# Value products in chunks of 128 tokens, with one chunk mixed from both batches

## The chip, the cores and the metric

The kernel runs on one core of a Trainium2 chip. The metric is the device time of one execution in microseconds (us), median of several runs. The engines are TensorE (PE, and PEld for its weight loads), VectorE (DVE), ScalarE (ACT), GpSimd (POOL) and SyncE (SP, which issues most DMAs). A matrix product has a stationary operand, which a weight load brings into the array (its columns become the partitions of the result), and a moving operand that streams past it (its columns become the columns of the result). Both are read over up to 128 partitions, the contraction.

## The reference, cut to what matters

Two batches of 448 tokens (`seq`) go through attention, then a block with a Fourier mixing and two dense layers, then the gated block that the change is about:

```python
def _moe2_ref(x, w_in, g_ln, w_sg, b_sg, w_out):        # x: (2, 448, 768)
    h = x @ w_in                                        # 768 -> 1024
    c = np.float32(np.sqrt(2.0 / np.pi))
    h = 0.5 * h * (1.0 + np.tanh(c * (h + 0.044715 * h ** 3)))
    d_ff = h.shape[-1]
    u, v = (h[..., :d_ff // 2], h[..., d_ff // 2:])     # 512 each
    mu = np.mean(v, axis=-1, keepdims=True)
    var = np.mean((v - mu) ** 2, axis=-1, keepdims=True)
    v_n = (v - mu) / np.sqrt(var + 1e-06) * g_ln
    v_s = np.einsum('ts,bsd->btd', w_sg, v_n) + b_sg[None, :, None]
    gated = u * v_s
    return (x + gated @ w_out).astype(np.float32)
```

The gate `w_sg` (448 by 448) mixes tokens, so `v_n` has to lie with tokens on partitions, while `u` and `x` lie with channels on partitions.

## The kernel before, in words

Every float32 product is made as three products: each operand is split into a high part that TensorE takes in one pass (`F32R`) and a rest, and `product()` (lines 134 to 141) adds high by high, high by rest and rest by high into one PSUM bank. So a contraction over `n` blocks is `3 n` weight loads and `3 n` matrix products.

The first 200 us hold attention and the Fourier block. Then line 1131 loops over six groups `g` of the dense layers: `hidden` (72 products of 448 columns a batch, "h") and `mixed` (72 a batch, "c"). In the last group `mixed` also splits its result into `x2[b]`, channels on partitions, six blocks of 448 tokens, high and rest. The gated block follows from line 1164:

- `gate_inputs(b)`: "u", four blocks of 128 channels, 18 products of 448 columns each; then the activation `gelu2`.
- `gate_values(b)`: "v", four chunks of 112 tokens (`CP`, `NT`). For each chunk 36 products: the stationary operand is the chunk's 112 tokens of `x2`, the moving one 256 columns of `w_in`. Then `gelu2`, mean and variance over the 512 channels, and the split into `vn[t]`, tokens on partitions. The six steps on VectorE and three on ScalarE of a chunk cover 112 partitions by 512 columns.
- `gate(b)`: "sg", four blocks `d` of 128 channels: 12 products each, contraction over the four chunks of 112 tokens, moving operand `sgT` (the gate, transposed and split, 112 partitions by 4 by 448). VectorE scales by `g_half`, adds `b_half` and multiplies by `ug[d]`; ScalarE and VectorE split that into `gated`.
- `project(b)`: "out", six blocks of 12 products, an add into `xT` on VectorE, four transposes "xt" a block, a copy on ScalarE and a DMA to the result.

Their order in the program is: u of batch 0, v of 0, u of 1, sg of 0, v of 1, `project` of 0 (six steps), sg of 1, the rest of `project` of 0, `project` of 1. A scheduler turns the program into one instruction order for each engine when the kernel is built; it may put an instruction that it expects to be ready ahead of one that it expects to wait. Engines then run their orders strictly, with semaphores between them. Dependences are followed for parts of a tile.

PSUM has eight banks. From line 992 on, four are two "big" tiles of two banks (only `hidden` uses them, through `big_ps`), and four form a ring that `one_ps` hands out in turn to everything else.

`sgT` is made in group 3 (lines 1146 to 1153): for each of four blocks of 112 rows of `w_sg` a DMA into the one buffer `sg_raw`, four transposes into a bank of the ring, and a split by ScalarE and VectorE into `sgT`. All four blocks share the one buffer, so each load after the first waits until the transposes of the block before have read it.

Of the kernel before, what the change touches and what calls it, by code (L numbers as in the profile page):

```python
# [12 lines left out]
F32 = mybir.dt.float32  # L13
F32R = mybir.dt.float32r
# [3 lines left out]
ALU = mybir.AluOpType  # L18
# [3 lines left out]
P = 128  # L22
B, H, S, D = 2, 12, 448, 64
C = H * D
NP = H // 2
CP = S // 4
NT = 4
FF1 = 4 * C
NF = FF1 // P
NG = 6  # L30
# [60 lines left out]
def attention_mixers_kernel(ctx, tc, bounded, q, k, v, cap, w_ch1, w_ch2, w_in, g_ln, w_sg, b_sg, w_out,  # L91
# [76 lines left out]

    xT = [keep.tile([P, NP, S], F32, name=f"xT{b}") for b in range(B)]
    normed = [None, None]  # L170


    def fourier(b, fp, t2sb, pool_folds=()):
# [83 lines left out]
    def layer_norm(b, fp):  # L257

        u = xT[b]

        def channel_sum(half, src, tag):
            vec.tensor_tensor(half, src[0], src[1], op=ALU.add)
            acc = fp.tile([P, S], F32, tag="acc", name=f"acc_{tag}{b}")
            vec.tensor_tensor(acc, half[:, 0, :], half[:, 1, :], op=ALU.add)
            vec.tensor_tensor(acc, acc, half[:, 2, :], op=ALU.add)
            return acc

        t = SimpleNamespace(d=[], sq=[])

        def total():  # L270
            half = fp.tile([P, 3, S + 2], F32, tag="y", bufs=2, name=f"half{b}")[:, :, :S]
            t.acc = channel_sum(half, (u[:, 0:3, :], u[:, 3:6, :]), "m")

        def mean():
            t.mu = two_ps(f"mu{b}", 1)[0]
            pe.matmul(t.mu[:, :S], mean_w, t.acc, start=True, stop=True)

        def centre():
            for i in range(2):
                d = fp.tile([P, 3, S], F32, tag="d", bufs=2, name=f"d{b}_{i}")  # L280
                vec.tensor_tensor(d, u[:, 3 * i:3 * i + 3, :], t.mu[:, :S].unsqueeze(1).to_broadcast([P, 3, S]),
                                  op=ALU.subtract)
                t.d.append(d)

        def square():
            for i in range(2):
                q2 = fp.tile([P, 3, S + 2], F32, tag="y", bufs=2, name=f"sq{b}_{i}")[:, :, :S]
                act.activation(q2, t.d[i], AF.Square)
                t.sq.append(q2)

        def square_total():
            t.acc2 = channel_sum(t.sq[0], t.sq, "v")

        def variance():
            t.vps = two_ps(f"var{b}", 1)[0]
            if bounded and not b:
                stream(t.vps, 12)
            for i in range(NT):
                pe.matmul(t.vps[:CP, 2 * i:2 * i + 2], t.acc2[:, i * CP:(i + 1) * CP], mean_w[:, 0:2],
                          start=True, stop=True)  # L300

        def deviation():
            var = small.tile([CP, NT], F32, tag="var", name=f"varc{b}")
            vec.tensor_scalar(var, t.vps[:CP, 0:2 * NT:2], 1e-6, None, op0=ALU.add)
            t.rstd = small.tile([CP, NT], F32, tag="rstd", name=f"rstd{b}")
            pool.tensor_tensor(t.rstd, var, neg_half[:CP, :NT], op=ALU.pow)

        def row():
            t.rps = two_ps(f"rstdrow{b}", 1)[0]
            if bounded and b:  # L310
                stream(t.rps, 12)
            for i in range(NT):
                pe.matmul(t.rps[:, i * CP:(i + 1) * CP], t.rstd[:, i:i + 1].to_broadcast([CP, P]), ident[:CP, :CP],
                          start=True, stop=True)

        def scale(c):
            part = lambda c: t.d[c // 3][:, c % 3, :]
            if c == 0:
                un[b] = normed[b].tile([P, 2, NP, S], F32R, tag="normed", name=f"un{b}")
            if c < NP:  # L320
                vec.tensor_tensor(part(c), part(c), t.rps[:, :S], op=ALU.mult)
            if 0 < c <= NP:
                act.copy(un[b][:, 0, c - 1, :], part(c - 1))
            if c > 1:
                vec.tensor_tensor(un[b][:, 1, c - 2, :], part(c - 2), f32(un[b][:, 0, c - 2, :]), op=ALU.subtract)  # L325

        return SimpleNamespace(total=total, mean=mean, centre=centre, square=square, square_total=square_total,
                               variance=variance, deviation=deviation, row=row, scale=scale)
# [466 lines left out]
    def gate_values(b, gp, x2, wv):  # L795

        vn = []

        def normalise(t, gv, mv):
            tc.keep_in_program_order(  # L800
                vec.tensor_scalar(gv, gv, mv[:, 0:1], mv[:, 1:2], op0=ALU.subtract, op1=ALU.mult))
            w = hpool[b].tile([P, 2, 512], F32R, tag="h", bufs=4, name=f"vn{b}_{t}")[:CP]
            split(w[:, 0], w[:, 1], gv)
            vn.append(w)

        last = None
        for t in range(NT):
            ps = one_ps(f"v{b}_{t}")
            for j in range(2):
                product(ps[:CP, j * 256:(j + 1) * 256], lambda n, a: x2[:, a, n, t * CP:(t + 1) * CP],  # L810
                        lambda n, a: wv[2 * j + n // 3][:, a, n % 3, :], NP)
            gv = gp.tile([P, DH], F32, tag="gv", bufs=3, name=f"gv{b}_{t}")[:CP]
            gelu2(gp, gv, ps[:CP, :], CP, f"v{b}_{t}", last)
            st = small.tile([P, 6], F32, tag="bst", name=f"bst{b}_{t}")[:CP]
            vec.bn_stats(st, gv)
            mv = small.tile([P, 2], F32, tag="bag", name=f"bag{b}_{t}")[:CP]
            vec.bn_aggr(mv, st)

            vec.tensor_scalar(mv[:, 1:2], mv[:, 1:2], 4e-6, None, op0=ALU.add)  # L819
            pool.tensor_tensor(mv[:, 1:2], mv[:, 1:2], neg_half[:CP, 0:1], op=ALU.pow)  # L820
            last = functools.partial(normalise, t, gv, mv)
        last()
        return vn

    def gate_inputs(b, gp, x2, wu):
# [6 lines left out]
            ug.append(g)  # L832
        return ug

    def gate(b, gp, vn, ug, sgT, g_half, b_half):
        gated = normed[b].tile([P, 2, ND, S], F32R, tag="normed", name=f"gated{b}")
        for d in range(ND):
            ps = one_ps(f"sg{b}_{d}")
            product(ps[:, :S], lambda n, a: vn[n][:, a, d * P:(d + 1) * P], lambda n, a: sgT[:, a, n, :], NT)
            tmp = gp.tile([P, S], F32, tag="gelu", bufs=3, name=f"gate{b}_{d}")  # L840
            vec.scalar_tensor_tensor(tmp, ps[:, :S], g_half[:, d:d + 1], b_half, op0=ALU.mult, op1=ALU.add)
            vec.tensor_tensor(tmp, tmp, ug[d], op=ALU.mult)
            split(gated[:, 0, d, :], gated[:, 1, d, :], tmp)
        return gated
# [279 lines left out]
    if not bounded:  # L1124
        run(mixed(1, 0, hs1, w2, None))
    sp_pool = ctx.enter_context(tc.tile_pool(name="spatial", bufs=1, side="right"))
    sgT = sp_pool.tile([CP, 2, NT, S], F32R, name="sgT", bufs=1)
    g_half = sp_pool.tile([P, GATE_ROW // 4], F32, name="g_half", bufs=1)[:, :ND]
    b_half = sp_pool.tile([P, S], F32, name="b_half", bufs=1)
    x2 = [None] * B  # L1130
    for g in range(1, NG):
        if g == 1:
            if bounded:
# [6 lines left out]
        else:  # L1140
            w1 = [columns(w_ch1, g * GF + f, "w1_") for f in range(GF)]
            hs = [[], []]
            for b in range(B):
                run(hidden(b, g, un, w1, hs[b]))
        if g == 3:
            for c in range(NT):
                sg_raw = sp_pool.tile([P, S], F32, tag="sgraw", bufs=1, name=f"sg_raw{c}")[:CP]
                sp.dma_start(sg_raw, w_sg[c * CP:(c + 1) * CP, :])
                ps = one_ps(f"sgT{c}")
                for t in range(NT):  # L1150
                    pe.transpose(ps[:CP, t * CP:(t + 1) * CP], sg_raw[:, t * CP:(t + 1) * CP], ident[:CP, :CP])
                src = ps[:CP, :S].rearrange("p (t x) -> p t x", t=NT)
                split(sgT[:, 0, :, c * CP:(c + 1) * CP], sgT[:, 1, :, c * CP:(c + 1) * CP], src)
            sp.dma_start(g_half, g_ln.rearrange("(n p) -> p n", p=P))
            vec.tensor_scalar_mul(g_half, g_half, 0.5)
            sp.dma_start(b_half, b_sg.unsqueeze(0).to_broadcast([P, S]))
            vec.tensor_scalar_mul(b_half, b_half, 0.5)
        w2 = [rows(w_ch2, g * GF + f, "w2_") for f in range(GF)]
        for b in range(B):
            if g == NG - 1:  # L1160
                x2[b] = normed[b].tile([P, 2, NP, S], F32R, tag="normed", name=f"x2_{b}")
            run(mixed(b, g, hs[b], w2, x2[b]))

    gp = ctx.enter_context(tc.tile_pool(name="gating", bufs=2, side="right"))
    wu = [columns(w_in, d, "wu") for d in range(ND)]
# [2 lines left out]
    for j in range(2):  # L1168
        for k in range(2):
            block = w_in[k * HC:(k + 1) * HC, 2 * DH + j * 512:2 * DH + (j + 1) * 512]  # L1170
            w = weight(f"wv{j}{k}", block.rearrange("(k p) f -> p k f", p=P), 3, 256, "wb")
            wv.append(w.rearrange("p a (k f) -> p a k f", k=3))
    vn0 = gate_values(0, gp, x2[0], wv)
    ug1 = gate_inputs(1, gp, x2[1], wu)
    gated0 = gate(0, gp, vn0, ug0, sgT, g_half, b_half)
    vn1 = gate_values(1, gp, x2[1], wv)
# [40 lines left out]
```

## Time and profile before

| | us |
|---|---|
| runs of the kernel before: median of 3 | 643.07 |
| lowest and highest | 642.69, 643.32 |
| span of the profiled execution | 641.1 |
| PE busy in it | 621.4 |
| VectorE busy | 502.7 |
| ScalarE busy | 273.5 |
| GpSimd busy | 82.9 |

The span goes from the first to the last instruction of the profiled execution; the runs time the whole execution, so they are somewhat above it. Busy time of PE includes the latency of each product and overlaps from product to product, so what a product costs in a stream is the distance from one to the next, not its duration. An engine's busy share says little alone: what matters is which engine the others wait for in a stretch.

### The profile page before, as it was taken

To read this page: it belongs to the slowest core of one execution; us is meant where nothing else is said; L and a number is where in the kernel's file an instruction comes from. 1 tells how busy PE (TensorE), PEld (TensorE's weight loads), DVE (VectorE), ACT (ScalarE), POOL (GpSimd) and SP (SyncE) were. 2 spreads that over 40 slices of the span, in tenths; PEclk is the share of its full clock that TensorE was granted. 3 is DMA by queue.
4 is the path that set the end of the run, shared out by engine and by line. 5 is a ranking of instruction groups with operands and counts; after the bars stand their busy time and mean duration, and the time that the engine had idled before them with its cause. 6 is when DMAs were issued, how large, how long until landed. Compare 5 with 4: busy or idle time off the path is not lost.

```text
span 641.1 us, 8759 instructions
## 1 busy us (share of the span) xinstructions
PE 621.4 (97%) x3414; PEld 536.5 (84%) x3414; DVE 502.7 (78%) x733; ACT 273.5 (43%) x374; POOL 82.9 (13%) x82
## 2 busy tenths in 40 slices
PE   7899999999999999999999999999999999999995
PEld 5444576559988999999999989999999999999995
DVE  1899999989985789998957882698589789997451
ACT  3998875671312244333403530352245244533121
POOL 1555564353000000000000000000000000101000
PEclk9999999999999999999999999999999999999998
DMA  6754820400401144544522360145054214000123
GB/s 164 185 135 102 244 61 15 139 0 2 147 2 28 50 147 154 174 157 138 167 99 70 128 204 32 48 151 173 23 153 143 99 50 149 1 1 1 44 58 78
DMA packets 69618, 62.74 MB, mean 98 GB/s; under 512 B 35840, under 2 KB 63296, under 8 KB 69568
## 3 DMA queue, kind: packets, MB, share of 16 engines
q1 hardware_dynamic: 68640, 61.86, 31.9%
q8 instruction: 29, 0.48, 0.3%
q10 hardware_dynamic: 928, 0.23, 0.2%
q14 instruction: 21, 0.17, 0.1%
HBM read 59.32 MB, written 2.75 MB: 97 GB/s over the span
## 4 chain that ended last, share of the span: by engine, by line
PE 83%; DVE 10%; DMA 2%; ACT 2%; issue 1%; POOLq 0%; POOL 0%; DVEq 0%; ACTq 0%; SPq 0%
PE c L140 26%; PE h L140 24%; PE v L140 5%; PE out L140 5%; PE u L140 4%; PE s L532 4%; PE o L556 4%; PE sg L140 3%; DVE r L576 2%; PE st L242 1%; DMA sg_raw<-in_moe_w_sg 1%; PE st L221 1%; PE tr L501 1%; ACT e L537 1%; PE idle L152 1%
## 5 line engine op out<-in xcount | busy, mean ns | idle before, releaser
L140 PE MATMUL h<-un,w 128*128 128x448 f32 x864 | 175.3, 363 | 0.5 <-DVE un L325 0.5
L140 PE MATMUL c<-h,w 128*128 128x448 f32 x864 | 175.4, 363 | 0.0
L140 PEld LDWEIGHTS h<-un,w 128*128 128x128 f32 x864 | 161.7, 188 | 12.4 <-DVE un L325 0.8
L140 PEld LDWEIGHTS c<-h,w 128*128 128x128 f32 x864 | 161.9, 188 | 11.1 <-issue 0.4
L736 DVE TENSOR_TENSOR xT<-xT,c 128x448 f32<-128x448 f32 x60 | 36.9, 617 | 37.2 <-PE c L140 37.2
L820 POOL TENSOR_TENSOR bag<-bag,neg_half 112x1 f32<-112x1 f32 x8 | 6.0, 745 | 396.5 <-DVE bag L819 396.5
L537 ACT ACTIVATE e<-s,tanh_scale 128x896 f32<-128x896 f32 (+1 forms) x48 | 41.1, 921 | 19.6 <-PE s L532 19.2
L556 PE MATMUL o<-e,v 128*64 128x448 f32 x192 | 41.1, 551 | 0.0
L541 ACT ACTIVATE e<-e,cap_pos 128x1792 f32<-128x1792 f32 (+1 forms) x24 | 37.7, 1620 | 0.0
L140 PE MATMUL v<-wv,x 128*112 128x256 f32 x288 | 34.2, 280 | 0.0
L140 PEld LDWEIGHTS v<-wv,x 128*112 128x112 f32 x288 | 34.1, 175 | 0.1
L727 ACT ACTIVATE h<-h 128x448 fp32r<-128x448 f32 x40 | 21.7, 542 | 28.7 <-DVE h L728 19.8
L532 PE MATMUL s<-qT,kT 64*128 64x448 f32 x216 | 27.5, 383 | 6.3 <-DVE qT L510 5.2
L576 DVE RECIPROCAL r<-den 128x448 f32<-128x448 f32 x11 | 32.4, 2948 | 0.8 <-PE den L569 0.7
L532 PEld LDWEIGHTS s<-qT,kT 64*128 64x128 f32 x216 | 19.3, 185 | 16.1 <-DVE qT L510 6.9
L140 PE MATMUL out<-gated,wo 128*128 128x448 f32 x144 | 30.8, 367 | 0.0
L140 PE MATMUL u<-x,wu 128*128 128x448 f32 x144 | 29.1, 362 | 0.0
L548 POOL TENSOR_TENSOR t<-t,e 128x896 f32<-128x896 f32 x12 | 28.6, 2381 | 0.8
L140 PEld LDWEIGHTS u<-x,wu 128*128 128x128 f32 x144 | 27.0, 188 | 1.8
L545 POOL TENSOR_TENSOR t<-e 128x896 f32<-128x896 f32 x12 | 27.8, 2320 | 2.7 <-POOL mix L521 1.7
L140 PEld LDWEIGHTS out<-gated,wo 128*128 128x128 f32 x144 | 26.4, 188 | 1.8 <-ACT res L861 0.2
L556 PEld LDWEIGHTS o<-e,v 128*64 128x64 f32 x192 | 11.8, 136 | 17.6 <-issue 15.2
(380 smaller groups left out, 900.7 us busy)
## 6 DMA issues: line engine op xcount, KB each, us to landing
k<-in_k SPq DMA_DIRECT2D x24, 112.0 KB, 2.8
out<-res SPq DMA_DIRECT2D x12, 224.0 KB, 2.5
q<-in_q SPq DMA_DIRECT2D x22, 112.0 KB, 2.8
t<-dft_channels SPq DMA_DIRECT2D x8, 291.0 KB, 5.1
v<-in_v SPq DMA_DIRECT2D x24, 96.0 KB, 2.3
w_0raw<-in_moe_w_ch SPq DMA_DIRECT2D x2, 768.0 KB, 5.0
w_1raw<-in_moe_w_ch SPq DMA_DIRECT2D x2, 768.0 KB, 6.0
w_2raw<-in_moe_w_ch SPq DMA_DIRECT2D x2, 768.0 KB, 4.7
```

The costliest lines, as they stand in the source:

```text
L140: pe.matmul(ps, lhs(i, a), rhs(i, b), start=start and m == 0, stop=stop and m == last)
L152: pe.matmul(ps[:, 0:2 * P], idle[:, 0:P], idle, start=True, stop=True)
L221: pe.matmul(ps[:HS, m * 256:m * 256 + NE], fold[:, i, m * HS:(m + 1) * HS], tab[:, i, :], start=i == 0, stop=i == 2)
L532: pe.matmul(ps[:, i, :S], t[lo:hi, x, at:at + P], qT[lo:hi, y, :], start=m == 0, stop=m == 2)
L537: act.activation(es[n][:, 2 * step:2 * step + nr], sums.pop((n, step))[:, :nr, :S], AF.Tanh, scale=tanh_scale)
L541: act.activation(part, part, AF.Exp, scale=cap_pos)
L545: pool.tensor_tensor(t, es[n][:, 0:2], es[n][:, 2:4], op=ALU.add)
L548: pool.tensor_tensor(ts[n], ts[n], es[n][:, 4:6], op=ALU.add)
L556: pe.matmul(os[n][halfs[j], :S], vts[n % 3][:, j, i], es[n][:, 2 * i + j if i < 3 else 6], start=i == 0, stop=i == 3)
L576: vec.reciprocal(r, den[:, :S])
L727: act.activation(h[:, 0], ps[:, i, :S], AF.Relu)
L736: vec.tensor_tensor(u[:, c, :], u[:, c, :], ps[:, :S], op=ALU.add)
```

## The change

Tokens are cut into three chunks of 128 (`NB`) and a rest of 64 for each batch. The rests of both batches share one chunk: `x2` of batch 0 gets 64 more columns for each block (`EXT` is 512), and two copies on GpSimd put the last 64 tokens of batch 1 there. `gate_values(0)` then makes four chunks of 128, the last one mixed; `gate_values(1)` makes three. `sgT` becomes 128 partitions by four blocks; the last block holds the columns 384 to 447 of `w_sg`, transposed, twice: on partitions 0 to 63 and again on 64 to 127. In `gate(0)` each block `d` begins with three pairs of products of 64 partitions: the lower half of the mixed chunk goes into batch 0's bank, the upper half into a bank of a "big" tile that is kept in `later` for batch 1. Nine products of 128 partitions follow. `gate(1)` has those nine alone and adds them to the kept bank. The rows of `w_sg` come in by two DMAs in group 2 into a tile of its own, and group 3 transposes from there. The constructor's `dynamic_dma_scratch_size` of 1024 leaves more on-chip memory to tiles.

```diff
+    wide = {}
+    def tokens(b, name):
+        t = normed[b].tile([P, 2, NP, S if b else EXT], F32R, tag="normed", name=f"{name}{b}")
+        wide[name, b] = t
+        return t[:, :, :, :S]
...
-        for t in range(NT):
+        for t in range(NB if b else NB + 1):
             ps = one_ps(f"v{b}_{t}")
             for j in range(2):
-                product(ps[:CP, j * 256:(j + 1) * 256], lambda n, a: x2[:, a, n, t * CP:(t + 1) * CP],
+                product(ps[:, j * 256:(j + 1) * 256], lambda n, a: x2[:, a, n, t * P:(t + 1) * P],
                         lambda n, a: wv[2 * j + n // 3][:, a, n % 3, :], NP)
...
+    later = []
     def gate(b, gp, vn, ug, sgT, g_half, b_half):
         for d in range(ND):
-            ps = one_ps(f"sg{b}_{d}")
-            product(ps[:, :S], lambda n, a: vn[n][:, a, d * P:(d + 1) * P], lambda n, a: sgT[:, a, n, :], NT)
+            if not b:
+                if d % 2 == 0:
+                    later.append(big_ps(f"sg1_{d}"))
+                ps = one_ps(f"sg{b}_{d}")
+                for m, (x, y) in enumerate(((0, 0), (0, 1), (1, 0))):
+                    for i, part in enumerate((ps, later[d // 2][:, d % 2])):
+                        half = slice(i * D, (i + 1) * D)
+                        pe.matmul(part[:, :S], vn[NB][half, x, d * P:(d + 1) * P], sgT[half, y, NB, :],
+                                  start=m == 0, stop=False)
+            else:
+                ps = later[d // 2][:, d % 2]
+            product(ps[:, :S], lambda n, a: vn[n][:, a, d * P:(d + 1) * P], lambda n, a: sgT[:, a, n, :], NB,
+                    start=False)
...
+        if g == 2:
+            raws_sg = ctx_sg.enter_context(tc.tile_pool(name="sg_rows", bufs=1))
+            sg_raw = raws_sg.tile([CP, NT, EXT], F32, name="sg_raw", bufs=1)
+            rows_sg = w_sg.rearrange("(c p) s -> p c s", c=NT)
+            sp.dma_start(sg_raw[:, :, :S], rows_sg)
+            sp.dma_start(sg_raw[:, :, S:], rows_sg[:, :, NB * P:])
         if g == 3:
-            for c in range(NT):
-                sg_raw = sp_pool.tile([P, S], F32, tag="sgraw", bufs=1, name=f"sg_raw{c}")[:CP]
-                sp.dma_start(sg_raw, w_sg[c * CP:(c + 1) * CP, :])
...
+            for n in range(NB + 1):
+                ps = one_ps(f"sgT{n}")
+                for c in range(NT):
+                    pe.transpose(ps[:, c * CP:(c + 1) * CP], sg_raw[:, c, n * P:(n + 1) * P], ident[:CP, :CP])
+                split(sgT[:, 0, n, :], sgT[:, 1, n, :], ps[:, :S])
+            ctx_sg.close()
...
+    for a in range(2):
+        pool.tensor_copy(wide["x2_", 0][:, a, :, S:EXT], x2[1][:, a, :, NB * P:])
...
-    vn0 = gate_values(0, gp, x2[0], wv)
+    vn0 = gate_values(0, gp, wide["x2_", 0], wv)
...
-    nc = bacc.Bacc("TRN2", target_bir_lowering=False, num_devices=1)
+    nc = bacc.Bacc("TRN2", target_bir_lowering=False, num_devices=1, dynamic_dma_scratch_size=1024)
```

## Rows read from the trace of the kernel before

**Rows 1.** Busy time by stretch: us, each engine's busy time (instructions), PEclk, DMA share, GB/s.

```profile
198.00:617.00 419.00, 418.07 (x2224) 392.71 (x2223) 327.78 (x513) 149.34 (x219) 5.96 (x8) 1.00 0.31 99
...
634.64:641.10 6.46, 0.00 (x1) 0.00 (x0) 0.00 (x0) 0.58 (x1) 0.00 (x0) 0.62 0.33 82
```

**Rows 2.** Chain that ended last, in order of time: start, us, what.

```profile
517.95 14.41 PE u L140 x72
532.36 16.92 PE v L140 x144
...
563.69 9.61 PE sg L140 x48
```

**Rows 3.** Groups by form: shapes, count, busy us, mean ns, idle before, releaser.

```profile
L1151 PE MATMUL sgT<-ident,sg_raw 112*112 112x112 f32 x16 | 2.3, 268 | 0.9 <-DMA sg_raw<-in_moe_w_sg 0.8
...
L140 PEld LDWEIGHTS v<-wv,x 128*112 128x112 f32 x288 | 34.1, 175 | 0.1
```

**Rows 4.** Timeline of weight loads ahead of short products: start, us, engine, operation, count.

```profile
133.12 0.86 PEld L299 LDWEIGHTS var<-mean_w,acc_v 128*112 128x112 f32 x8
...
135.65 0.97 PEld L313 LDWEIGHTS rstdrow<-ident,rstd 112*128 112x128 f32 x8 [0.70 <-POOL rstd L306]
```

**Rows 5.** Timeline of attention's products of 64 partitions, and their neighbours on PE.

```profile
12.55 0.77 PE L532 MATMUL s<-qT,kT 64*128 64x448 f32 x6
13.30 0.85 PE L532 MATMUL s<-qT,mix 128*128 128x448 f32 x3
...
63.77 0.55 PE L569 MATMUL den<-t,ones 128*64 128x448 f32 x2
64.25 2.12 PE L532 MATMUL s<-qT,kT 64*128 64x448 f32 x18
```

**Rows 6.** Timeline of the end: gate of batch 1, then its projection.

```profile
605.71 9.85 PE L140 MATMUL sg<-sgT,vn 112*128 112x448 f32 x48
...
608.46 0.68 DVE L841 SCALAR_TENSOR_TENSOR gate<-sg,g_half,b_half 128x448 f32<-128x448 f32 x1 [2.29 <-PE sg L140]
...
610.98 0.68 DVE L841 SCALAR_TENSOR_TENSOR gate<-sg,g_half,b_half 128x448 f32<-128x448 f32 x1
...
616.83 5.05 PE L140 MATMUL out<-gated,wo 128*128 128x448 f32 x24
...
617.97 0.63 DVE L132 TENSOR_TENSOR gated<-gate,gated 128x448 fp32r<-128x448 f32 x1 [0.63 <-ACT gated L131]
```

**Rows 7.** Timeline of VectorE in the gate of batch 0.

```profile
568.73 0.62 DVE L842 TENSOR_TENSOR gate<-gate,ug 128x448 f32<-128x448 f32 x1
569.26 0.67 DVE L841 SCALAR_TENSOR_TENSOR gate<-sg,g_half,b_half 128x448 f32<-128x448 f32 x1
...
570.72 0.61 DVE L132 TENSOR_TENSOR gated<-gate,gated 128x448 fp32r<-128x448 f32 x1
```

**Rows 8.** Last write of batch 1's x2 (timeline), and two of POOL's groups by form.

```profile
519.86 0.62 DVE L132 TENSOR_TENSOR x<-xT,x 128x448 fp32r<-128x448 f32 x1
...
L191 POOL TENSOR_TENSOR y<-xT 128x448 f32<-128x448 f32 x4 | 4.9, 1250 | 4.8 <-DVE xT L577 4.8
...
L521 POOL CAST mix<-kT 64x128 fp32r<-64x128 f32 x12 | 3.5, 292 | 0.7
```

**Rows 9.** SP's queue: a fetch of group 2, and the first wait of sg_raw's loads.

```profile
269.70 0.34 SPq L670 DMA_DIRECT2D w_8raw<-in_moe_w_ch  x1
...
374.67 4.02 SPq L1148 DMA_DIRECT2D sg_raw<-in_moe_w_sg  x2
```

**Rows 10.** Timelines: a tile read part by part; PE's first products, and later ones.

```profile
197.68 3.08 PE L140 MATMUL h<-un,w 128*128 128x448 f32 x14 [0.53 <-DVE un L325]
...
200.21 0.62 DVE L325 TENSOR_TENSOR un<-d,un 128x448 fp32r<-128x448 f32 x1
...
3.31 5.11 PE L152 MATMUL idle<-ident 128*128 128x256 bf16 x24 [3.31 <-POOL ident masks.py:199]
...
15.00 1.47 PE L152 MATMUL s<-ident 128*128 128x256 bf16 x12
```

More of the change, by code (lines that the diff above doesn't have):

```diff
@@ L27 @@
 NT = 4
+NB = S // P
+EXT = NB * P + P
 FF1 = 4 * C
@@ L318, in scale @@
             if c == 0:
-                un[b] = normed[b].tile([P, 2, NP, S], F32R, tag="normed", name=f"un{b}")
+                un[b] = tokens(b, "un")
             if c < NP:
@@ L801, in normalise @@
                 vec.tensor_scalar(gv, gv, mv[:, 0:1], mv[:, 1:2], op0=ALU.subtract, op1=ALU.mult))
-            w = hpool[b].tile([P, 2, 512], F32R, tag="h", bufs=4, name=f"vn{b}_{t}")[:CP]
+            w = hpool[b].tile([P, 2, 512], F32R, tag="h", bufs=4, name=f"vn{b}_{t}")
             split(w[:, 0], w[:, 1], gv)
@@ L806, in gate_values @@
         last = None
-        for t in range(NT):
+        for t in range(NB if b else NB + 1):
             ps = one_ps(f"v{b}_{t}")
             for j in range(2):
-                product(ps[:CP, j * 256:(j + 1) * 256], lambda n, a: x2[:, a, n, t * CP:(t + 1) * CP],
+                product(ps[:, j * 256:(j + 1) * 256], lambda n, a: x2[:, a, n, t * P:(t + 1) * P],
                         lambda n, a: wv[2 * j + n // 3][:, a, n % 3, :], NP)
-            gv = gp.tile([P, DH], F32, tag="gv", bufs=3, name=f"gv{b}_{t}")[:CP]
-            gelu2(gp, gv, ps[:CP, :], CP, f"v{b}_{t}", last)
-            st = small.tile([P, 6], F32, tag="bst", name=f"bst{b}_{t}")[:CP]
+            gv = gp.tile([P, DH], F32, tag="gv", bufs=3, name=f"gv{b}_{t}")
+            gelu2(gp, gv, ps, P, f"v{b}_{t}", last)
+            st = small.tile([P, 6], F32, tag="bst", name=f"bst{b}_{t}")
             vec.bn_stats(st, gv)
-            mv = small.tile([P, 2], F32, tag="bag", name=f"bag{b}_{t}")[:CP]
+            mv = small.tile([P, 2], F32, tag="bag", name=f"bag{b}_{t}")
             vec.bn_aggr(mv, st)
             vec.tensor_scalar(mv[:, 1:2], mv[:, 1:2], 4e-6, None, op0=ALU.add)
-            pool.tensor_tensor(mv[:, 1:2], mv[:, 1:2], neg_half[:CP, 0:1], op=ALU.pow)
+            pool.tensor_tensor(mv[:, 1:2], mv[:, 1:2], neg_half[:, 0:1], op=ALU.pow)
             last = functools.partial(normalise, t, gv, mv)
@@ L1126, in attention_mixers_kernel @@
     sp_pool = ctx.enter_context(tc.tile_pool(name="spatial", bufs=1, side="right"))
-    sgT = sp_pool.tile([CP, 2, NT, S], F32R, name="sgT", bufs=1)
+    sgT = sp_pool.tile([P, 2, NB + 1, S], F32R, name="sgT", bufs=1)
     g_half = sp_pool.tile([P, GATE_ROW // 4], F32, name="g_half", bufs=1)[:, :ND]
@@ L1130, in attention_mixers_kernel @@
     x2 = [None] * B
+    ctx_sg = ExitStack()
     for g in range(1, NG):
@@ L1144, in attention_mixers_kernel @@
                 run(hidden(b, g, un, w1, hs[b]))
-        if g == 3:
-            for c in range(NT):
-                sg_raw = sp_pool.tile([P, S], F32, tag="sgraw", bufs=1, name=f"sg_raw{c}")[:CP]
-                sp.dma_start(sg_raw, w_sg[c * CP:(c + 1) * CP, :])
[L1149 to L1153, printed above, removed]
+        if g == 2:
[4 more added lines that the diff above has]
+            sp.dma_start(sg_raw[:, :, S:], rows_sg[:, :, NB * P:])
+        if g == 3:
+            for n in range(NB + 1):
[4 more added lines that the diff above has]
+            ctx_sg.close()
             sp.dma_start(g_half, g_ln.rearrange("(n p) -> p n", p=P))
@@ L1160, in attention_mixers_kernel @@
             if g == NG - 1:
-                x2[b] = normed[b].tile([P, 2, NP, S], F32R, tag="normed", name=f"x2_{b}")
+                x2[b] = tokens(b, "x2_")
             run(mixed(b, g, hs[b], w2, x2[b]))
+    for a in range(2):
+        pool.tensor_copy(wide["x2_", 0][:, a, :, S:EXT], x2[1][:, a, :, NB * P:])
     gp = ctx.enter_context(tc.tile_pool(name="gating", bufs=2, side="right"))
```

## The prediction

> **What bounds the kernel now.** I first asked for busy time by stretch. [...] The chain of waits then gives what a product costs in a stream: u, 14.41 us for 72 products of 448 columns, is 200 ns each; sg, 9.61 us for 48, is the same 200 ns although only 112 partitions are filled; v, 16.92 us for 144 products of 256 columns, is 117.5 ns [rows 2].
>
> The span is 641.1 us and the median of the runs 643.07, 2.0 us (0.3%) more, which lies around the span; I make the sum on the span and carry those 2.0 us over unchanged.
>
> **The transposes of the gate.** The two loads go out two groups earlier, into a tile of their own, and the four old loads leave SP's queue. The 0.9 us of waiting goes: -0.9. What is late next is nothing I can see: the loads should go out near 269.70 us, ahead of the group's second-layer weights [rows 9], some 100 us before the transposes. Those weights are passed by two issues of 0.3 to 0.4 us and one more transfer; their products begin only after the group's 144 "h" products of 200 ns, so 28.8 us hide that. Sixteen transposes stay sixteen; each stationary block has 128 columns instead of 112, at the same 112 moving ones, so I take no difference. Four banks of the ring are now asked for within some 1.6 us; if their split is late, PE waits up to 1 us.
>
> **The value products.** Seven chunks instead of eight: 36 of 288 products go, at 117.5 ns: -4.23 us. This holds only if a product with 128 stationary columns still takes 117.5 ns. PEld is busy in all of v (34.1 us in 33.8, idle 0.1) [rows 3], which looks as if loads were the limit; but a load lasts 175 ns and they overlap, so this says nothing on their pace. Their pace stands where the products are shorter than the loads: eight loads of 112 columns take 0.86 us, which is (0.86-0.18)/7 = 97 ns each, and eight of 128 columns 0.97 us, 111 ns each [rows 4]. Both are under 117.5 ns, so moving columns set the pace of v, now and afterwards: 252 products, 29.6 us instead of 33.84. The upper bound is that each product grows by the 14 ns of its load: 252 times 131.5 is 33.1 us, a gain of 0.7 instead of 4.2. I take the lower one, since rows show such a load at 111 ns. VectorE and ScalarE lose one chunk of eight; that is off the path.
>
> The two copies on POOL move 384 elements a partition each. The nearest rows are 0.29 us (128 elements) and 1.25 us (an add of 448) [rows 8], so 0.6 to 2.5 us for both; I take 2. They start at the last write of batch 1's `x2`, at 520.5 us [rows 8], and the mixed chunk is read at 532.36 + 3 times 4.23 = 545.0 us: 22 us of cover. Behind them on POOL wait only the powers of the first chunk, after 536 us.
>
> **The gate products.** Before: 96 products, 19.2 us. After: 72 full ones and 12 pairs. Attention has pairs of exactly this form: 18 products in nine pairs take 2.12 us; less the last one's 0.36 us, and 0.12 at the start, these are eight steps of 0.20 [rows 5]. So a pair costs 200 ns, like one product, and 12 products' worth goes: -2.4 us. But the array changes its form. Going in: after "den" (its last pair due 0.37 us after 63.77) the first pair comes 0.1 us late, and the second another 0.1: 0.2 us. Going out: the last pair of the six at 12.55 starts at 12.96; the next product was due at 13.16, came at 13.30, and the three after it take 0.85 us where 0.77 was due: again 0.2 [rows 5]. Eight changes, in and out for each of four blocks, cost 8 times 0.2 = +1.6 us (bounds 0.1 and 0.3 each: 0.8 to 2.4). Together -0.8. The split of this matters: batch 0's gate gets 1.6 us longer, batch 1's 2.4 us shorter.
>
> [...]
>
> The kept banks are the two "big" tiles, unused since the last `hidden`. Batch 0's gate needs the mixed chunk first, not last; between its last product and the gate lie, as before, the 14.4 us of u [rows 2], three times a chunk's own 4.2.
>
> **What is late next.** At the end batch 1's gate meets VectorE. Before, the scalings of consecutive blocks start at 608.46 and 610.98: 2.5 us, because VectorE waits 0.63 us for ScalarE's half of the split before its own; the last `gated` is done at 618.60, and PE, in "out" from 616.83, needs it for its tenth product, at 616.83 + 1.8 = 618.63 [rows 6]. So before it just fits. After, PE comes 2.4 us sooner (10.5 us after the gate's start), and the first scaling 0.6 us sooner (2.15). If VectorE keeps its order, the last `gated` comes at 2.15 + 3 times 2.5 + 2.6 = 12.3: PE waits 1.8. If the scheduler puts the next scaling into the gap, as it did for batch 0 (569.26 stands between 568.73 and 570.72) [rows 7], a block costs VectorE's own 0.68 + 0.62 + 0.63 = 1.93 and small gaps, and the end comes near 11.2: PE waits 0.7. If PE's order is filled with the next block's products, 0. I take 0.7, as the next scaling is ready (3.95) before ScalarE is done (4.1): +0.7.
>
> **Sum.** -0.9 - 4.2 - 0.8 + 0.7 = -5.2 us: span 635.9, median 637.9.
>
> **The rivals.**
> - *Loads set the pace of v.* Then 252 products cost up to 131.5 ns: gain 0.7 instead of 4.2, time 638.9 to 641.4. For it: PEld without a gap [rows 3]. Against it: 111 ns [rows 4]. [...]
> - *Pairs don't overlap*, the change does not do what it says: 12 more steps of 200 ns, 640.3. Against it: attention's pairs, of the same 64 by 128 by 448.
> - *The copies hold up u.* If u of batch 0 waits for the copies into its tile (they write columns between those it reads), PE stands from 517.8 to 522.5 us, 4.7 us: 642.6, no change to speak of. Against it: "h" ran on `un` from 197.68 while VectorE wrote later parts of that tile at 200.21 [rows 10], so waits go by parts; but those parts did not interleave.
> - *The same, and the clock falls in that pause*: this is the slower case. [...] After its first idle stretch PE took 5.11 us for 24 short products; later 12 took 1.47, which makes 24 about 2.8 [rows 10]: 2.3 us lost. 637.9 + 4.7 + 2.3 = 644.9. It is slower as soon as pause and clock cost over 5.2 + 1.3 us.
> - *A new instruction order* that makes PE wait for a bank or weights somewhere in 320 us of dense layers: several us, 641 to 644. Nothing in the rows speaks for it but that the tiles and sizes have changed.
>
> **How the numbers follow.** A measurement of this kernel can tell 0.2%, 1.3 us, from no change. Forecast 0.66, 636.8 to 639.0 (changes of form 0.15 to 0.3 us each, the wait at the end 0 to 1.8); loads 0.11; pairs 0.05; u held up 0.06; held up with a lower clock 0.04; new order 0.08, most of it within 0.2%. Faster is the first three, 0.82, and a little of the last: 0.83; same 0.13; slower 0.04. The range has to leave out no more than 2 in 10: 636.4 to 641.0 takes in the forecast, the pairs and most of the loads.
>
> **What would show it.** In the profile after: v at 117 to 118 ns for 252 products (131 if loads set the pace); pairs of sg at 200 ns and 0.2 us lost on either side; no PE wait by `sg_raw`; u of batch 0 following "c" without a gap; a PE wait of some 0.7 us ahead of the tenth "out" product of batch 1, or VectorE's order changed there. The prediction is wrong if PE gets a gap before 600 us, or if v's products grow.

## The result, and the profile after

The changed kernel takes 636.80 us (median of 4 runs, 635.89 to 636.98), the kernel before 642.88 (median of 4, 641.09 to 643.32): ratio 0.9909, 95% interval 0.9894 to 0.9925. The profiled execution's span went from 641.1 to 635.0 us. The forecast was 637.9, within 636.4 to 641.0, faster.

Busy time by stretch of the changed kernel (us, each engine's busy time, then clock, DMA share, GB/s). PE has no idle time at all from 198 to 615 us, where 0.93 us was idle before [rows 1]:

```profile
198.00:615.00 417.00, 417.00 (x2209) 389.49 (x2210) 325.78 (x507) 148.30 (x218) 6.39 (x9) 1.00 0.31 101
```

The groups by form of the changed kernel answer to [rows 3]: the transposes wait for nothing, and the loads of v now last 188 ns.

```profile
L142 PE MATMUL v<-wv,x 128*128 128x256 f32 x252 | 29.7, 279 | 0.0
...
L142 PEld LDWEIGHTS v<-wv,x 128*128 128x128 f32 x252 | 29.7, 188 | 0.1
...
L1178 PE MATMUL sgT<-ident,sg_raw 112*128 112x112 f32 x16 | 1.7, 259 | 0.0
```

The chain that ended last of the changed kernel, in order of time (start, us, what), answers to [rows 2]:

```profile
370.87 1.54 PE sgT L1178 x16
...
516.67 14.41 PE u L142 x72
531.08 16.80 PE v L142 x144
547.88 14.41 PE u L142 x72
562.29 0.81 PE sg L856 x5
563.10 2.02 PE sg L142 x9
...
573.56 12.61 PE v L142 x108
586.17 9.61 PE out L142 x48
...
601.91 5.52 PE sg L142 x27
607.43 1.31 PE xt L881 x12
608.74 2.00 PE sg L142 x9
610.74 4.97 PE out L142 x24
...
628.58 0.59 ACT res L883
```

From the starts in this chain and in that of before, stretch by stretch:

| stretch | before, us | after, us | difference | forecast |
|---|---|---|---|---|
| first transposes of `w_sg` to u of batch 0 | 147.26 | 145.80 | -1.46 | -0.9 |
| u of both batches | 28.82 | 28.82 | 0 | 0 |
| v of batch 0 (144 products) | 16.92 | 16.80 | -0.12 | 0 |
| gate of batch 0 | 9.61 | 11.27 | +1.66 | +1.6 |
| v of batch 1 (144, then 108 products) | 16.92 | 12.61 | -4.31 | -4.23 |
| "out" of batch 0 up to the gate of batch 1 | 15.74 | 15.74 | 0 | 0 |
| gate of batch 1 to the last copy | 28.76 | 26.67 | -2.09 | -1.7 |

These sum to -6.3; the first 370 us of the changed kernel's execution were 0.2 us longer. In the traces of this case the dense layers start up to 1.4 us apart, and the last DMA ends 4.6 to 5.8 us after the last copy, whichever kernel it is. So I compare stretches below, which repeat within 0.1 us where the code is the same, and spans only beside them.

### The profile page after: what moved, and what is told of

Read it like the earlier page. It is cut to its first block, busy times and chain, and to the rows that moved or that the text cites. A ratio compares the mean times of both kernels' runs of the same rounds, so it can differ in the third digit from the quotient of the medians.

```text
span 635.0 us, 8681 instructions
## 1 busy us (share of the span) xinstructions
PE 616.4 (97%) x3378; PEld 529.3 (83%) x3378; DVE 498.8 (79%) x725; ACT 271.5 (43%) x371; POOL 83.4 (13%) x83
## 4 chain that ended last, share of the span: by engine, by line
PE 86%; DVE 10%; ACT 1%; issue 1%; DMA 1%; POOLq 0%; POOL 0%; DVEq 0%; ACTq 0%; SPq 0%
PE c L142 26%; PE h L142 25%; PE v L142 5%; PE out L142 5%; PE u L142 5%; PE s L541 4%; PE o L565 4%; PE sg L142 2%; DVE r L585 2%; PE st L251 2%; PE tr L510 1%; PE st L230 1%; PE den L578 1%; ACT e L546 1%; PE idle L154 1%
## 5 line engine op out<-in xcount | busy, mean ns | idle before, releaser
L1191 POOL CAST x<-x 128x384 fp32r<-128x384 f32 x2 | 1.3, 672 | 324.6 <-ACT x L133 324.0
L142 PE MATMUL v<-wv,x 128*128 128x256 f32 x252 | 29.7, 279 | 0.0
L142 PEld LDWEIGHTS v<-wv,x 128*128 128x128 f32 x252 | 29.7, 188 | 0.1
```

The lines of the kernel that those rows point to most:

```text
L142: pe.matmul(ps, lhs(i, a), rhs(i, b), start=start and m == 0, stop=stop and m == last)
```

## The experiments

**The array's changes of form.** The pairs' saving and the loss at a change of form come as one sum in the table (+1.66 -2.4 in the two gates). Three kernels take them apart. The first turns the order in blocks 0 and 2 of batch 0's gate:

```diff
+                ahead_of = d % 2 == 1
+                if not ahead_of:
+                    full(True, False)
                 for m, (x, y) in enumerate(((0, 0), (0, 1), (1, 0))):
...
+                if ahead_of:
+                    full(False, True)
...
```

> The changed kernel, with the order turned in every second block of batch 0's gate: blocks 0 and 2 take the nine full products first and then the pairs, blocks 1 and 3 the pairs first. So the pairs of two blocks are neighbours and the array changes its form four times instead of eight. Theory (each change costs 0.2 us, going in and going out alike): the gate of batch 0 goes from 11.26 to 10.46 us, the span from 635.0 to 634.2. Rival (what is lost belongs to each block's three pairs, however they lie): the gate stays at 11.26, the span at 635.0.

Measured: PE's timeline of the changed kernel, and below it of this one, with start, us and count. The first row ends the stretch before the gate, the last begins the stretch that follows it.

```profile
558.73 3.57 PE L142 MATMUL u<-x,wu 128*128 128x448 f32 x17
562.23 0.88 PE L856 MATMUL sg<-sgT,vn 64*128 64x448 f32 x6
563.03 2.08 PE L142 MATMUL sg<-sgT,vn 128*128 128x448 f32 x9
565.05 0.88 PE L856 MATMUL sg<-sgT,vn 64*128 64x448 f32 x6
...
573.40 3.78 PE L142 MATMUL v<-wv,x 128*128 128x256 f32 x31
```

```profile
559.66 2.37 PE L142 MATMUL u<-x,wu 128*128 128x448 f32 x11
561.87 1.97 PE L142 MATMUL sg<-sgT,vn 128*128 128x448 f32 x9
563.76 1.48 PE L861 MATMUL sg<-sgT,vn 64*128 64x448 f32 x12
...
572.31 1.92 PE L142 MATMUL v<-wv,x 128*128 128x256 f32 x15
```

By this view the gate takes 573.40 - 562.23 = 11.17 us in the changed kernel and 572.31 - 561.87 = 10.44 here. But part of the first change lies ahead of the gate's first row: u's products are 0.20 us apart, so after the 17 from 558.73 the first pair was due at 562.13 and came at 562.23, 0.10 late. Here full products follow u, due at 561.86 after the 11 from 559.66, and they come at 561.87. With that 0.10 the changed kernel's gate is the 11.27 us of the table, so it is 0.83 us for four changes fewer, 0.21 each. All other stretches agree within 0.05 us; the span is 633.9. The loss belongs to the change of form, not to the pairs.

The second keeps the chunks of 128 and drops the pairs:

```diff
-                for m, (x, y) in enumerate(((0, 0), (0, 1), (1, 0))):
...
+            product(ps[:, :S], lambda n, a: vn[n][:, a, d * P:(d + 1) * P],
+                    lambda n, a: sgT[:, a, NB + b if n == NB else n, :], NB + 1)
...
+        pool.memset(f32(sgT[D:P, a, NB, :]), 0.0)
+        pool.memset(f32(sgT[0:D, a, NB + 1, :]), 0.0)
...
```

> The changed kernel without pairs: the mixed chunk stays, but the gate's last block of sgT exists twice, once with the upper and once with the lower 64 partitions set to zero, and each batch's gate has twelve full products a block again (96 in all instead of 72 and 12 pairs). Theory (pairs save 2.4 us of products and lose 1.6 at the changes of form): batch 0's gate 9.6 us (-1.66), batch 1's end longer by 2.1, the time that it had gained there; span 635.4, at most 635.8. Rival (the changes of form cost nothing that counts): 2.4 us more, 637.4.

Measured, from the chain of this kernel:

```profile
561.30 9.61 PE sg L142 x48
570.91 12.72 PE v L142 x108
...
599.39 9.61 PE sg L142 x48
...
615.32 0.44 PE xt L871 x4
```

Batch 0's gate is back at 9.61 us, 1.66 less than the 11.27 of the table, and from the start of batch 1's gate to the first transposes of its projection it takes 2.12 us longer than in the changed kernel (599.39 to 615.32 us in this chain, 601.91 to 615.72 in that one). So the pairs are worth 2.12 - 1.66 = 0.46 us net, as the theory says (0.4), and not 2.4. Apart from that, v of batch 1 takes 0.11 us longer: 117.8 ns for each of its 108 products instead of 116.7, although its stationary blocks have the same 128 columns; no run here shows why. The span, 634.2, is below the changed kernel's 635.0 only because this execution's first 370 us were 1.0 us shorter and its last DMA ended 0.4 us sooner after the last copy.

The third asks whether two halves run at once only as neighbours:

```diff
-                for m, (x, y) in enumerate(((0, 0), (0, 1), (1, 0))):
-                    for i, part in enumerate((ps, later[d // 2][:, d % 2])):
+                for i, part in enumerate((ps, later[d // 2][:, d % 2])):
+                    for m, (x, y) in enumerate(((0, 0), (0, 1), (1, 0))):
```

> The changed kernel, but the six products of 64 partitions in a block run as three of the lower half and then three of the upper half, instead of alternating. Theory (two run at once only as neighbours on different halves, so only the third and the fourth overlap): five steps of 200 ns instead of three in each of four blocks, +1.6 us, gate of batch 0 12.86 us, span 636.6. Rival one (the array overlaps them whatever their order): 11.26 and 635.0. Rival two (nothing overlaps in this order): 6 steps, +2.4 us, 637.4.

Measured: 0.81 us from the first product of 64 partitions to the first full one, as in the changed kernel (562.23 to 563.03), and 2.82 us for the whole first block, as there (562.23 to 565.05). The scheduler kept the order of the edit: three products of the lower half stand ahead of three of the upper half among PE's instructions. My theory was wrong.

```profile
562.56 0.88 PE L856 MATMUL sg<-sgT,vn 64*128 64x448 f32 x6
563.37 2.08 PE L142 MATMUL sg<-sgT,vn 128*128 128x448 f32 x9
565.38 0.88 PE L856 MATMUL sg<-sgT,vn 64*128 64x448 f32 x6
```

This leaves two readings: each half takes its own products, however they are ordered, or a product of 64 partitions takes 100 ns alone. The next kernel leaves the upper half's three products out:

```diff
-                    for i, part in enumerate((ps, later[d // 2][:, d % 2])):
+                    for i, part in enumerate((ps,)):
...
-                    start=False)
+                    start=bool(b))
```

> The changed kernel without the upper half's products: batch 0's gate runs three products of 64 partitions a block, one after the other in one half of the array, instead of six, and the last 64 tokens of batch 1 are left out of its gate, which is a part of the computation. It is to settle why six such products took three steps of 200 ns even when three of one half were issued ahead of three of the other. Theory one (each half takes its own products as they come, 200 ns each): batch 0's gate stays at 11.2 us. Theory two (a product of 64 partitions takes 100 ns by itself): 4 blocks times 0.3 us less, 10.0.

Measured: three products take the same time as six, 0.81 us up to the first full one, and the first block 2.82 us. So a product of 64 partitions costs 200 ns (0.81 us for three, with 0.21 for the change of form in it), and the other half's run beside it, even if three of one half are issued ahead of three of the other.

```profile
561.41 0.88 PE L856 MATMUL sg<-sgT,vn 64*128 64x448 f32 x3
562.22 2.09 PE L142 MATMUL sg<-sgT,vn 128*128 128x448 f32 x9
564.23 0.87 PE L856 MATMUL sg<-sgT,vn 64*128 64x448 f32 x3
```

**The early load alone**, in the kernel before:

```diff
+            sp.dma_start(sg_raw, w_sg.rearrange("(c p) s -> p c s", c=NT))
...
-                sg_raw = sp_pool.tile([P, S], F32, tag="sgraw", bufs=1, name=f"sg_raw{c}")[:CP]
-                sp.dma_start(sg_raw, w_sg[c * CP:(c + 1) * CP, :])
...
```

> The kernel before with one part of the change alone: the rows of w_sg come by one DMA in group 2 into a tile of their own, and group 3 transposes from there (blocks of 112 as before). Between the two kernels the stretch from the first of these transposes to u of batch 0 fell from 147.25 to 145.80 us, 1.45 in place of the 0.9 of waiting that I had counted. Theory (the early load alone does it, and the 0.5 beyond the waiting are weight loads that could not start ahead): the stretch is 145.8 us here too, the span 1.45 less than before, 639.7. Rival (0.9 belongs to the loads, 0.5 to the 128-column transposes or to a new order): 146.35.

Measured: 145.81 us in this stretch where the kernel before took 147.25. The early load gives all of it, and the 128-column transposes nothing. (The span, 638.2, is 1.5 below the expected 639.7: the last DMA ended 1.2 us sooner after the last copy than before, and the first 370 us were 0.2 shorter.) In the trace the 16 transposes now stand in one run:

```profile
370.30 1.70 PE L1154 MATMUL sgT<-ident,sg_raw 112*112 112x112 f32 x16
```

**The layout alone**, in the kernel before:

```diff
+EXT = NB * P + P
...
+        return normed[b].tile([P, 2, NP, S if b else EXT], F32R, tag="normed", name=f"{name}{b}")[:, :, :, :S]
...
+    nc = bacc.Bacc("TRN2", target_bir_lowering=False, num_devices=1, dynamic_dma_scratch_size=1024)
```

> The kernel before with its data laid out as in the change and nothing else: batch 0's un and x2 in rows of 512 columns, of which 448 are used, and the small DMA scratch, which moves every tile. Theory (the place and the pitch of an operand don't touch the pace): u, v and sg take 14.41, 16.92 and 9.61 us as before, the span stays at 641.1 within the 0.5 us by which the first 200 us differ from run to run. Rival (v went from 117.5 to 116.7 ns a product because of the layout): v of batch 0 takes 16.80 us here.

Measured: u, v and sg as before, span 641.5. The layout costs nothing, and v's 116.7 ns is not its doing. From this kernel's chain:

```profile
518.60 14.41 PE u L142 x72
533.01 16.92 PE v L142 x144
```

**u held up by the copies**, the slower rival, built into the changed kernel:

```diff
-        pool.tensor_copy(wide["x2_", 0][:, a, :, S:EXT], x2[1][:, a, :, NB * P:])
+        tc.keep_in_program_order(
+            pool.tensor_copy(wide["x2_", 0][:, a, :, S:EXT], x2[1][:, a, :, NB * P:]))
+    for a in range(2):
+        own = wide["x2_", 0][:, a, :, NB * P:S]
+        tc.keep_in_program_order(pool.tensor_copy(own, own))
```

> The changed kernel with the rival of the prediction built in: after the two copies GpSimd copies 64 columns of batch 0's x2 onto themselves, so u of batch 0 has to wait until the copies are done. Theory one (PE pauses from 516.5 us for the last split, four copies, some 4.9 us, and its clock holds): u starts at 521.4, span 639.9. Theory two (the clock falls in that pause): the first products of u take 400 ns instead of 200 for some microseconds, 2.3 us more, 642.2. If u does not wait, the span stays near 635.0 and the premise is wrong.

Measured: 641.8 us of span. PE's timeline, and then busy time by stretch (PE, PEld, DVE, ACT, POOL, PEclk, DMA share, GB/s):

```profile
521.46 17.27 PE L142 MATMUL u<-x,wu 128*128 128x448 f32 x72 [4.50 <-POOL x L1195]
...
538.57 1.68 PE L142 MATMUL v<-wv,x 128*128 128x256 f32 x13
```

```profile
521.00:525.00 4.00, 3.54 (x9) 2.98 (x10) 4.00 (x6) 0.00 (x0) 1.19 (x2) 0.50 0.00 0
525.00:529.00 4.00, 4.00 (x17) 3.63 (x16) 2.29 (x4) 1.67 (x3) 0.00 (x0) 0.75 0.64 233
529.00:533.00 4.00, 4.00 (x22) 3.75 (x21) 2.99 (x6) 2.34 (x4) 0.00 (x0) 1.00 0.42 164
```

From the first transposes of `w_sg` to u it takes 4.67 us longer than in the changed kernel, and u takes 17.10 us (538.57 less 521.46) instead of 14.41, as the granted clock is 0.50 from 521 to 525 us, where nine products take 3.54 us, 393 ns each: 7.4 us together (the span is 6.8 longer, as its last DMA ended 0.9 us sooner after the last copy and its first 370 us were 0.3 longer). Theory two holds. The price that I had worked out was 4.7 + 2.3 = 7.0. In the changed kernel itself, PE worked through that moment without a gap (4.00 us busy from 517 to 521 us, at a granted clock of 1.00), as "c" is followed by u there.

**The kept banks.** In the changed kernel's batch 1, PE doesn't run the gate's blocks in order: the transposes of batch 0 stand ahead of the last nine products, and these start only when VectorE has scaled the block before, whose bank lies in the same two-bank tile:

```profile
607.93 0.68 DVE L863 SCALAR_TENSOR_TENSOR gate<-sg,g_half,b_half 128x448 f32<-128x448 f32 x1
...
608.66 1.71 PEld L142 LDWEIGHTS sg<-sgT,vn 128*128 128x128 f32 x9 [0.17 <-DVE gate L863]
```

Dealt out the other way, neighbours share no tile:

```diff
-                if d % 2 == 0:
+                if d < 2:
...
-                    for i, part in enumerate((ps, later[d // 2][:, d % 2])):
+                    for i, part in enumerate((ps, later[d % 2][:, d // 2])):
...
```

> The changed kernel, with the kept banks dealt out the other way: blocks 0 and 2 in one two-bank tile, 1 and 3 in the other, so that neighbours never share a tile. In the changed kernel the products of block 1 of batch 1's gate wait for VectorE's scaling of block 0, which reads the other bank of the same tile, and PE's order was rearranged around that. Theory (this wait costs its two late weight loads and a later last scaling): from the start of batch 1's gate to the first transposes of its projection 13.5 us instead of 13.9, span 634.6. Rival (VectorE's chain sets the end anyway): 13.9 and 635.0.

Measured: 13.53 us instead of 13.89 from the start of the gate to the first transposes of the projection. PE's 36 products run in one piece, and VectorE puts the next scaling into the gap before its half of the split:

```profile
601.57 7.46 PE L142 MATMUL sg<-sgT,vn 128*128 128x448 f32 x36
...
615.10 0.60 PE L881 MATMUL xt<-ident,xT 128*112 128x128 f32 x4
```

```profile
605.53 0.68 DVE L863 SCALAR_TENSOR_TENSOR gate<-sg,g_half,b_half 128x448 f32<-128x448 f32 x1 [0.46 <-PE sg L142]
606.13 0.62 DVE L134 TENSOR_TENSOR gated<-gate,gated 128x448 fp32r<-128x448 f32 x1
```

**Both lessons in one kernel:**

```diff
+                banks_of.append(one_ps(f"sg{b}_{d}"))
...
+            product(banks_of[d][:, :S], lambda n, a: vn[n][:, a, d * P:(d + 1) * P], lambda n, a: sgT[:, a, n, :], NB,
+                    start=not b, stop=bool(b))
...
+        if not b:
+            for d in range(ND):
+                for m, (x, y) in enumerate(((0, 0), (0, 1), (1, 0))):
...
```

> The changed kernel with both lessons put in: batch 0's gate runs the full products of all four blocks first and then all twelve pairs, so that the array changes its form twice instead of eight times, and the kept banks are dealt out so that neighbouring blocks of batch 1's gate never share a tile. Theory (0.18 us a change, 0.36 at the end, both measured apart): batch 0's gate 10.0 us instead of 11.17, the end 13.5 instead of 13.9, span 1.5 less than the changed kernel's, 633.4, and some 1.2% below the kernel before. Rival (banks come free later, as VectorE scales four blocks at once, and v of batch 1 waits): the gate gains 1.2 and v loses up to that.

Measured: 634.47 us (634.27 to 634.77), 0.9885 of the kernel before (641.33 beside these runs), interval 0.9867 to 0.9902; span 632.9. In PE's timeline the gate of batch 0 is two runs, 9.91 us, and v of batch 1 takes 12.71 (12.61 in the changed kernel, where no change stands right ahead of v): no bank is late. Together that is 22.62 us where the changed kernel took 11.27 + 12.61 = 23.88, 1.26 for six changes fewer, again 0.21 each and not the expected 0.18. The end is 13.53 us, 0.36 less.

```profile
562.25 7.37 PE L142 MATMUL sg<-sgT,vn 128*128 128x448 f32 x36
569.55 2.68 PE L871 MATMUL sg<-sgT,vn 64*128 64x448 f32 x24
572.16 4.00 PE L142 MATMUL v<-wv,x 128*128 128x256 f32 x32
```

## Why the prediction was right, point by point

**What bounds the kernel.** From 198 to 617 us PE has next to no gap [rows 1], so that removed products count in full: shown, by the stretches that did not change and by v of batch 1, which lost 36 products and 4.31 us.

**The value products.** I took 117.5 ns for a product with 128 stationary columns, against an upper bound of 131.5. Measured are 16.80 us for 144, 116.7 ns. The rival in which loads set the pace is gone: the loads last 188 ns now instead of 175, and the products came no slower. It was right to read the pace of loads from products shorter than a load [rows 4], and not from PEld's busy share, which is full in v in both kernels. Why a product became 0.8 ns cheaper is open: the layout alone left it at 117.5, and the 128 columns alone don't do it either, as the kernel without pairs has 116.7 ns in v of batch 0 and 117.8 in v of batch 1.

**The gate products.** Pairs at 200 ns and 0.2 us at each change of form came from attention's rows [rows 5]; +1.66 us was measured for +1.6, and 0.21 us for a change in the two kernels where the number of changes was varied (the 0.18 in the last expectation leaves out the 0.10 us ahead of the first pair). The rival in which pairs don't overlap is gone by the kernel with three products in place of six.

**The transposes.** The term was too small: -0.9 forecast, -1.46 measured, and the early load alone gives -1.44. The step that failed is the reading of idle time. I took the 0.9 us that the profile gives as idle before these instructions [rows 3]. But that is counted from the end of the product before, and a product of 363 ns is followed by the next after 200: it ends some 0.16 us after its successor could have begun. Each of three stops loses that as well, 0.5 us together. PE's timeline of the kernel before has the three stops:

```profile
372.74 0.97 PE L140 MATMUL h<-un,w 128*128 128x448 f32 x4
374.05 0.60 PE L1151 MATMUL sgT<-ident,sg_raw 112*112 112x112 f32 x4 [0.34 <-DMA sg_raw<-in_moe_w_sg]
...
376.11 1.17 PE L140 MATMUL c<-h,w 128*128 128x448 f32 x5
377.74 0.60 PE L1151 MATMUL sgT<-ident,sg_raw 112*112 112x112 f32 x4 [0.46 <-DMA sg_raw<-in_moe_w_sg]
...
379.80 1.17 PE L140 MATMUL c<-h,w 128*128 128x448 f32 x5
381.10 0.59 PE L1151 MATMUL sgT<-ident,sg_raw 112*112 112x112 f32 x4
```

At 0.20 us a product the transposes were due at 373.54, 377.11 and 380.80 us, and they came 0.51, 0.63 and 0.30 late: 1.44 us, which is what the early load gave. The held-up u shows the same: 4.50 us idle by its row, 4.67 lost. The loads also went out otherwise than I had read from [rows 9]: one group ahead and not two, at 248.48 and 249.75 us, 122 us before the transposes.

**The end.** I took 0.7 us of waiting before the tenth "out" product, as VectorE would be late; 0.3 was lost (2.09 of 2.4 us came through). The mechanism was another, so it is luck that some wait stood where one was forecast. The forecast order of VectorE appears only when the kept banks are dealt out differently, and then next to nothing is lost (13.53 us, where 16.00 - 2.4 = 13.6 was to be had). In the changed kernel neighbouring blocks wait for each other, since the scheduler's waits treat the two banks of one such tile as one; that dependences are followed for parts of a tile, as I wrote of the kernel before, doesn't hold there. PE's order was also filled with products of the next "out" block ahead of the tenth, the case for which I had put no wait. I had looked at which tiles the banks come from, but not at who shares a tile.

**The copies on POOL** were hidden, as forecast: the two take 0.57 and 0.78 us and end near 520.3, ahead of the mixed chunk by more than 20 us. The slower rival did not happen, as waits went by parts of a tile here even where the parts interleave (u began at 516.67 us, the first copy at 518.46); its price was about right (7.4 us for 7.0).

**What was off in sum.** -5.2 forecast, -6.1 by the spans: 0.6 from the transposes, 0.4 from the end, 0.2 from v, less 0.1 in batch 0's gate and the 0.2 us of the first part. The larger misses went one way: 636.80 us lies at the lower edge of the 636.8 to 639.0 that my own terms allowed.

## What to carry to other kernels

Where TensorE has no gap, count products (36 fewer in v were 4.31 us here), and read the pace of a product or a load from a stream of its own kind; busy shares and durations of overlapping instructions don't give it (v's loads lasted 188 ns, and its products came every 116.7). Products of 64 partitions on different halves ran two at a time here (six in the 0.81 us of three alone), but each change of form cost 0.21 us, so put all of them into one run, as the last kernel does. When banks are kept for later, don't let neighbours in the order of work share a tile (0.36 us here).

## What the runs showed of the hardware that was not expected

Products of 64 partitions on different halves of the array did not have to alternate: six products issued as three of one half and then three of the other took the same three steps of 200 ns as three alone, 0.81 us up to the first full product in both kernels.

Steps of VectorE were longer while POOL copied. In the changed kernel two of them that overlap the copies take 0.93 and 0.86 us, where their kind takes 0.62 (as the same step does at 519.86 in the kernel before, without a copy [rows 8]) and 0.55. The step between them overlaps the second copy by 0.4 us and takes its usual 0.55, and that copy takes 0.78 us where the first took 0.57; why this step isn't slowed is not shown. In the kernel with u held up the copies take 0.57 and 0.77 us. Timeline of VectorE and POOL in the changed kernel:

```profile
518.46 0.57 POOL L1191 CAST x<-x 128x384 fp32r<-128x384 f32 x1 [324.02 <-ACT x L133]
518.58 0.93 DVE L134 TENSOR_TENSOR x<-xT,x 128x448 fp32r<-128x448 f32 x1
519.43 0.55 DVE L697 TENSOR_SCALAR wv10cvt<-wv10cvt 128x768 f32<-128x768 f32 x1
519.57 0.78 POOL L1191 CAST x<-x 128x384 fp32r<-128x384 f32 x1 [0.54 <-DVE x L134]
519.90 0.86 DVE L697 TENSOR_SCALAR wv11cvt<-wv11cvt 128x768 f32<-128x768 f32 x1
```

A pause of TensorE of 4.67 us cost 2.7 us more afterwards: the granted clock was 0.50 from 521 to 525 us, after the pause, and 1.00 again from 529 us on.
